# Ordering ScalarE and VectorE by a build-time clock model, with a whole-bank copy and later store transposes

## The chip, the core and the metric

The kernel runs on one core of a Trainium2 chip. Its engines are TensorE (PE, matmuls; PEld is its weight load), VectorE (DVE), ScalarE (ACT), GpSimd (POOL) and SyncE (SP, which here only issues DMAs). Each engine takes its instructions strictly in the order in which the program lists them, and waits on semaphores for the others. The metric is the time of one execution on the device, in microseconds.

## What is computed

```python
# x: (4, 4096, 192) -> 16384 tokens of 192 numbers
out = einsum(softmax(weight) over 7 taps, x padded in front)   # causal, per head
x1 = square(relu(out @ moe_w_in)) @ moe_w_out                  # d_ff = 2048
h2 = x1 @ moe2_w_in
y  = maximum(0.01 * h2, h2) @ moe2_w_out
```

A short convolution over the sequence is followed by two feed-forward layers of the same shape. Layer 1 has relu and square between its matrix products, layer 2 a leaky relu.

## The kernel before

**Tiles and steps.** The 16384 tokens are 32 tiles of 512 (`TT`). A *step* is one layer, one tile and one pair of 128-wide slices of d_ff: `steps[s] = (u, p)` with `u = (layer, tile)` and p from 0 to 7. There are 512 steps. Up to step 47 the kernel also decodes the weights; from step 48 (`THREE`) all steps have one pattern, and from step 64 a period of 32 steps repeats: 16 of layer 1 (two tiles of 8 steps), then 16 of layer 2 for the same two tiles.

**Numbers in two parts.** Matmuls run in a reduced format, so every operand is held as a high and a low part: `hi` is the rounded value, `lo` what is left. From step 48 on, both low parts of a pair are also added up (`both`, made by `add_low`, L619), which saves a matmul.

**What a step does.** TensorE makes two `h` banks of the step (18 matmuls) and, in three blocks of six between them, the 18 output matmuls of step s-2 (`LAG = 2`). Each matmul uses 64 of the 128 rows, and two run side by side, so a step is 18 pairs: five pairs of `h`, three of outputs, two of `h`, three of outputs, two of `h`, three of outputs. ScalarE applies the activation twice (`act`, L576 or L578), squares one of the two in layer 1 (`square`, L585) and rounds both (`high`, L603). VectorE squares the other (L583), takes both differences (`low`, L607) and adds them (`add_low`, L619). The output matmuls of step s, two steps later, need `hi`, `lo` and `both`; for even p of an even tile, and odd p of an odd one, the matmul with `both` stands in the first block of three pairs, otherwise in the second (`g2_one`, order `turn`).

**Leaving the banks.** A tile's outputs gather in three of four PSUM banks: M holds 128 of the 192 columns, E and F hold the rest, each half of it for the wrong half of the partitions. When a tile's last output matmuls have been listed (the `alone` case, `evac_one`), ScalarE copies both halves of E (L743, L744) and half of F (L747), and VectorE adds the rest (`add_rest`, L750) and later the main part (`add_main`, L753) into the scratch tile `ring`. The next tile takes the free bank as M, E as its F and F as its E. Its first matmul into the old E stands at the sixth pair of the step after the leaving one, and into the old F at the eleventh.

**Fill-in work.** VectorE also makes the convolution (`xT` transposes L411, taps L433 and L435 into `acc`), the operands of later tiles (`x`, L484) and the transposes of finished tiles for the stores (`y`, L763, L768), each followed by four store DMAs on SP's queue (L797). These stand in queues `prep` and `leave`, each piece with a due step. `pieces` (L1052) takes from them as long as a budget of VectorE time per step lasts (`STEP`, `SHORT`, `budget`), at most two (`many`) a step, and one around a leaving. The main loop calls it between the activations and the rounding of each step, and after a leaving keeps `both` of the step before back (`pending`) until the leaving's instructions stand.

## Time and profile before

| | |
|---|---|
| median of 3 runs | 2125.22 us (2124.95 to 2126.22) |
| the profiled execution | 2129.57 us |
| its span on the core | 2127.9 us |
| TensorE busy | 2080.6 us, 98% |
| VectorE busy | 1641.3 us, 77%, 2575 instructions |
| ScalarE busy | 1469.1 us, 69%, 2700 instructions |
| mean granted TensorE clock | 0.995 of full speed |

The page of the profile gives one execution. TensorE is busy nearly all the time, yet busy time hides small waits, since two matmuls run side by side and a waiting one still counts beside its neighbour. So it is the length of the steps that is to be read: the time from the first `h` matmul of one step to that of the next, which the timeline of TensorE shows, and the length of a stretch of 16 steps that has been cut at such matmuls.

### The profile page before, as it was taken

The numbers are of one execution on the slowest core, as the hardware profiler recorded it, in microseconds if no ns is written. First come the engines' busy times: TensorE is split into PE (matmuls) and PEld (weight loads), VectorE is DVE, ScalarE is ACT, GpSimd is POOL, SyncE is SP. The second block draws the span as 40 slices with busy tenths as digits, with TensorE's granted clock in tenths as the row PEclk, the third lists the DMA queues.
The fourth block names the chain that finished last, engine by engine and source line by source line (L and its number), as shares of the span: only waits on it lengthen the run. The fifth ranks groups of instructions, "written<-read, shape, count | busy, mean of one in ns | idle before, by whom it ended". The sixth has DMA issues, their size and how long they took to land.

```text
span 2127.9 us, 46893 instructions
## 1 busy us (share of the span) xinstructions
PE 2080.6 (98%) x18592; PEld 1946.0 (91%) x18592; DVE 1641.3 (77%) x2575; ACT 1469.1 (69%) x2700; POOL 61.4 (3%) x114
## 2 busy tenths in 40 slices
PE   9999989999999999999999999999999999999998
PEld 5799988999989999898999989999999998989998
DVE  8787768787777878778787787877778787787764
ACT  7787657667676776767667676676767667677674
POOL 2201210000000000000000000000000000000000
PEclk9999999999999999999999999999999999999999
DMA  8531131121212112131121211212121121311110
GB/s 189 145 95 36 24 57 26 40 37 46 39 23 48 29 46 42 20 65 26 36 39 32 51 26 39 38 45 39 24 48 28 46 42 21 65 21 41 24 33 16
DMA packets 232677, 95.07 MB, mean 45 GB/s; under 512 B 203208, under 2 KB 218696, under 8 KB 232456
## 3 DMA queue, kind: packets, MB, share of 16 engines
q1 hardware_dynamic: 229288, 88.90, 21.2%
q0 software_dynamic: 1168, 2.75, 0.6%
q8 instruction: 145, 2.38, 0.5%
q14 instruction: 76, 0.62, 0.1%
q10 hardware_dynamic: 2000, 0.42, 0.1%
HBM read 25.19 MB, written 12.58 MB: 18 GB/s over the span
## 4 chain that ended last, share of the span: by engine, by line
PE 66%; DVE 22%; ACT 7%; issue 4%; DMA 1%; SPq 0%; DVEq 0%; POOL 0%; ACTq 0%
PE h L544 32%; PE o1m L544 12%; PE o0r L544 11%; PE o1r L544 7%; DVE lo L607 6%; PE o0m L544 5%; DVE both L619 4%; DVE g L583 4%; ACT hi L603 3%; DVE acc_b L435 1%; DVE acc_a L435 1%; DVE ring L750 1%; ACT ring L743 1%; ACT zs L744 1%; ACT ring L747 1%
## 5 line engine op out<-in xcount | busy, mean ns | idle before, releaser
L544 PE MATMUL h<-x,w 64*128 64x512 f32 x9216 | 1350.0, 377 | 2.1 <-ACT g L578 0.9
L544 PEld LDWEIGHTS h<-x,w 64*128 64x128 f32 x9216 | 1038.0, 186 | 23.4 <-ACT g L578 1.3
L607 DVE TENSOR_TENSOR lo<-g,hi 128x512 fp32r<-128x512 f32 x1022 | 661.6, 688 | 325.7 <-ACT hi L603 295.6
L603 ACT CAST hi<-g 128x512 fp32r<-128x512 f32 x1020 | 581.5, 620 | 192.0 <-DVE g L583 188.3
L544 PE MATMUL o1m<-hi,w 64*128 64x512 f32 x2044 | 623.3, 382 | 0.5 <-DVE ring L750 0.5
L544 PE MATMUL o0r<-hi,w 64*128 64x512 f32 x1948 | 586.9, 379 | 0.0
L578 ACT ACTIVATE g<-h 128x512 f32<-128x512 f32 x512 | 279.6, 595 | 320.5 <-PE h L544 319.8
L544 PE MATMUL o1m<-both,w 64*128 64x512 f32 x926 | 360.2, 389 | 25.6 <-DVE both L619 24.5
L544 PE MATMUL o0r<-lo,w 64*128 64x512 f32 (+1 forms) x1022 | 383.6, 378 | 0.0
L544 PEld LDWEIGHTS o1m<-hi,w 64*128 64x128 f32 x2044 | 358.1, 186 | 22.3 <-DVE ring L750 0.9
L544 PEld LDWEIGHTS o0r<-hi,w 64*128 64x128 f32 x1948 | 342.7, 186 | 23.5 <-ACT zs L744 3.2
L619 DVE TENSOR_TENSOR both<-lo 128x512 fp32r<-128x512 f32 x463 | 319.9, 691 | 15.0
L544 PE MATMUL o0m<-hi,w 64*128 64x512 f32 x1088 | 324.8, 379 | 1.6 <-DMA hi<-g 1.6
L544 PE MATMUL o1r<-hi,w 64*128 64x512 f32 x1052 | 322.1, 381 | 0.2 <-ACT zs L744 0.2
L576 ACT ACTIVATE g<-h 128x512 f32<-128x512 f32 x512 | 277.3, 591 | 60.1 <-PE h L544 59.3
L544 PEld LDWEIGHTS o1m<-both,w 64*128 64x128 f32 x926 | 172.2, 186 | 64.3 <-DVE both L619 61.5
L544 PE MATMUL o0m<-lo,w 64*128 64x512 f32 x560 | 208.8, 377 | 0.0
L544 PE MATMUL o1r<-lo,w 64*128 64x512 f32 (+1 forms) x526 | 201.8, 384 | 6.0 <-DVE lo L607 6.0
L544 PEld LDWEIGHTS o0m<-hi,w 64*128 64x128 f32 x1088 | 192.3, 186 | 3.9 <-DMA hi<-g 2.0
L544 PEld LDWEIGHTS o1r<-hi,w 64*128 64x128 f32 x1052 | 186.7, 186 | 4.1 <-ACT zs L744 0.6
L544 PEld LDWEIGHTS o0r<-lo,w 64*128 64x128 f32 (+1 forms) x1022 | 187.0, 183 | 3.6
L585 ACT ACTIVATE g<-g 128x512 f32<-128x512 f32 x269 | 169.0, 631 | 7.8
(136 smaller groups left out, 1333.4 us busy)
## 6 DMA issues: line engine op xcount, KB each, us to landing
x<-x SPq DMA_DIRECT2D x189, 256.0 KB
out_dram<-y SPq DMA_DIRECT2D x186, 64.0 KB
raw_a<-in_x_dram SPq DMA_DIRECT2D x127, 64.0 KB
raw_b<-in_x_dram SPq DMA_DIRECT2D x62, 64.0 KB
lent<-in_moe_w_out_dram SPq DMA_DIRECT2D x13, 256.0 KB
lent<-in_moe_w_in_dram SPq DMA_DIRECT2D x13, 192.0 KB
lent<-in_moe_w_in_dram SPq DMA_DIRECT2D x13, 128.0 KB
lent<-in_moe_w_out_dram SPq DMA_DIRECT2D x13, 128.0 KB
```

Of the source, the lines that this page charges most:

```text
L435: nc.vector.scalar_tensor_tensor(out=acc[0], in0=src, scalar=w, in1=acc[0], op0=ALU.mult, op1=ALU.add)
L544: return nc.tensor.matmul(out=o.rearrange("p (b a) -> p b a", a=2), lhsT=w, rhs=z.rearrange("p (a b) -> p b a", a=2), start=begin, stop=end_,)
L576: nc.scalar.activation(out=g, in_=hps.pop((u, f)), func=ACTF.Relu)
L578: nc.scalar.activation(out=g, in_=hps.pop((u, f)), func=ACTF.Prelu, alpha=0.01)
L583: nc.vector.tensor_mul(out=g, in0=g, in1=g)
L585: nc.scalar.activation(out=g, in_=g, func=ACTF.Square)
L603: nc.scalar.copy(out=a, in_=gsp[u, f])
L607: nc.vector.tensor_sub(out=b, in0=gsp.pop((u, f)), in1=f32(hi[u, f]))
L619: nc.vector.tensor_add(out=c, in0=f32(lo[u, 2 * p]), in1=f32(lo[u, 2 * p + 1]))
L743: nc.scalar.copy(out=z3[w], in_=E[v])
L744: nc.scalar.copy(out=got["s"][v], in_=E[w])
L747: nc.scalar.copy(out=z3[v], in_=F[w])
```

## The change

The order of ScalarE's and VectorE's instructions from step 48 on (the 49th) no longer comes from the budget but from a function `single`. It keeps one clock for each of the two engines, in nanoseconds, and a time `begun` at which TensorE would begin the step if it never waited (18 pairs of 215.6). It knows when `h`, E and F would be ready, lists the step's chain of instructions with 545 on ScalarE, 615 on VectorE and 70 from one to the next, and before every VectorE instruction of the chain calls `fill`, which takes pieces from the same queues as long as the chain's end, `both`, stays before `by`, a time 250 ahead of its matmul; a piece that is not due is taken only if the chain's end moves by no more than 40.

Beside this, `both` belongs to the chain of its own step and is no longer held back. E is copied whole, with one ScalarE instruction in place of two, and F's half goes straight to its place in `ring`; `add_main` is two VectorE instructions of 64 partitions in place of one of 128. The leaving's copies stand between the activations. The store transposes of layer 2 are due two steps later than before (`LEAVE + 2`), though a piece may be taken early.

```diff
+PAIR = 215.6
+STEP_ = 18 * PAIR
+ON_A, ON_D, LATENCY = 545, 615, 70
...
         def early():
-            got["s"] = f32(stage.tile([P, NW], I32, tag="m", name="zs")[:, 0:TT])
-            nc.scalar.copy(out=z3[w], in_=E[v])
-            nc.scalar.copy(out=got["s"][v], in_=E[w])
+            nc.scalar.copy(out=z3, in_=E)
 
         def other():
-            nc.scalar.copy(out=z3[v], in_=F[w])
+            nc.scalar.copy(out=z[v], in_=F[w])
 
         def add_rest():
-            nc.vector.tensor_add(out=zr[v], in0=F[v], in1=got["s"][v])
+            nc.vector.tensor_add(out=zr[v], in0=F[v], in1=z3[w])
 
         def add_main():
-            nc.vector.tensor_add(out=z, in0=M, in1=z3)
+            nc.vector.tensor_add(out=z[w], in0=M[w], in1=z3[v])
+            nc.vector.tensor_add(out=z[v], in0=M[v], in1=z[v])
...
+        def fill(s, chain, at, by, scalar=0):
+
+            while True:
+                best = None
+                for q in (leave, prep, dec):
+                    if not q or (q[0][3] and not q[0][3]()):
+                        continue
+                    cost = q[0][1]
+                    if cost < 0 and not scalar:
+                        continue
+                    if cost > 0:
+                        end = ends(chain, cost, at)
+                        if end > (by if q[0][0] <= s else min(by, ends(chain, 0, at) + 40)):
+                            continue
...
+        def single(s, begun, A, Z, leaving, then, alone):
...
+            at = {"h": begun + 5 * PAIR + 2 * (3 + COVER) * PAIR + 300}
+            first = min(j for order in turns_of(p) for j, k in enumerate(order) if k == (1 if (u[1] % 2 == 0) else 2))
+            by = begun + 2 * STEP_ + (5 + 3 * first + COVER * first + 2) * PAIR - 250
+            names = ("actZ", "actA") if l == 1 else ("actA", "actZ")
+            chain = [(names[0], "A", ON_A, ("h",)), (names[1], "A", ON_A, ("h",))]
+            if l == 1:
+                chain += [("sqZ", "D", ON_D, ("actZ",)), ("sqA", "A", ON_A, ())]
+            chain += [("hiA", "A", ON_A, ("actA",)), ("hiZ", "A", ON_A, ("sqZ", "actZ"))]
+            chain += [("loA", "D", ON_D, ("hiA",)), ("loZ", "D", ON_D, ("hiZ",)), ("c", "D", ON_D, ("loZ",))]
...
+            if alone:
+                early, other, add_rest = leaving
+                at["E"], at["F"] = begun + STEP_ - 3 * PAIR + 300, begun + STEP_ + 300
+                chain = [("e", "A", ON_A, ("E",)), chain[0], ("f", "A", ON_A, ("F",)), ("z", "D", ON_D, ("F", "e"))] + chain[1:]
...
+            if three:
+                begun += STEP_
...
+                then = single(s, begun, A, Z, leaving, then if leaving else (), alone)
+                release()
+                if leaving:
+                    own = (2, u2[1]) if u2[0] == 1 else None
+                    wait = LEAVE if u2[0] == 1 else LEAVE + 2
...
-                if three:
-                    (pending.append if soon else lambda fn: fn())(lambda u=u, p=p: add_low(u, p))
```

TensorE's order of instructions is the same in both kernels. VectorE lists 60 instructions more and ScalarE 60 fewer.

**VectorE at a leaving in layer 1.** Steps 128 and 129 (step 129 is a leaving one), from just behind the `xT_b` transpose. `g` is the square, `lo` the differences, `ring<-o0r` is `add_rest`, `ring<-o1r` is `add_main`, `acc_b` a tap. Before:

```order
L583 TENSOR_TENSOR g<-g 128x512
L433 TENSOR_SCALAR acc_b<-xT_b,taps 128x512
L435 SCALAR_TENSOR_TENSOR acc_b<-xT_b,taps,acc_b 128x512
L607 TENSOR_TENSOR lo<-g,hi 128x512 x2
L750 TENSOR_TENSOR ring<-o0r,zs 64x512
L619 TENSOR_TENSOR both<-lo 128x512
L583 TENSOR_TENSOR g<-g 128x512
L435 SCALAR_TENSOR_TENSOR acc_b<-xT_b,taps,acc_b 128x512
L607 TENSOR_TENSOR lo<-g,hi 128x512 x2
L619 TENSOR_TENSOR both<-lo 128x512
L753 TENSOR_TENSOR ring<-o1r,ring 128x512
L763 STREAM_TRANSPOSE y<-ring 128x512
```

Now:

```order
L435 TENSOR_SCALAR acc_b<-xT_b,taps 128x512
L585 TENSOR_TENSOR g<-g 128x512
L609 TENSOR_TENSOR lo<-g,hi 128x512 x2
L621 TENSOR_TENSOR both<-lo 128x512
L437 SCALAR_TENSOR_TENSOR acc_b<-xT_b,taps,acc_b 128x512 x2
L750 TENSOR_TENSOR ring<-o0r,ring 64x512
L585 TENSOR_TENSOR g<-g 128x512
L609 TENSOR_TENSOR lo<-g,hi 128x512 x2
L621 TENSOR_TENSOR both<-lo 128x512
L753 TENSOR_TENSOR ring<-o1r,ring 64x512
L754 TENSOR_TENSOR ring<-o1r,ring 64x512
```

`both` of step 128 has moved from behind `add_rest` to before two taps and `add_rest`, and the store transpose has moved away from here, to step 132.

**ScalarE at the same place.** `ring<-o1m` is the copy of E, `ring<-o0r` that of F's half, `g<-h` the activations, `hi` the rounding. Before:

```order
L603 CAST hi<-g 128x512 x2
L743 COPY ring<-o1m 64x512
L744 COPY zs<-o1m 64x512
L747 COPY ring<-o0r 64x512
L576 ACTIVATE g<-h 128x512 x2
L585 ACTIVATE g<-g 128x512
```

Now:

```order
L744 COPY ring<-o1m 128x512
L578 ACTIVATE g<-h 128x512
L747 COPY ring<-o0r 64x512
L578 ACTIVATE g<-h 128x512
L587 ACTIVATE g<-g 128x512
L605 CAST hi<-g 128x512 x2
```

One copy has gone, and the first activation has moved ahead of F's copy.

**VectorE at the first store transpose of tile 2 of layer 2, steps 58 and 59.** `ring<-o0m` is `add_main`, `y` the store transpose, whose tile is one buffer that the stores of the tiles before still read. Before:

```order
L619 TENSOR_TENSOR both<-lo 128x512
L753 TENSOR_TENSOR ring<-o0m,ring 128x512
L763 STREAM_TRANSPOSE y<-ring 128x512
L607 TENSOR_TENSOR lo<-g,hi 128x512 x2
L619 TENSOR_TENSOR both<-lo 128x512
L435 SCALAR_TENSOR_TENSOR acc_a<-xT_a,taps,acc_a 128x512 x2
```

Now:

```order
L621 TENSOR_TENSOR both<-lo 128x512
L753 TENSOR_TENSOR ring<-o0m,ring 64x512
L754 TENSOR_TENSOR ring<-o0m,ring 64x512
L609 TENSOR_TENSOR lo<-g,hi 128x512 x2
L621 TENSOR_TENSOR both<-lo 128x512
L764 STREAM_TRANSPOSE y<-ring 128x512
L486 TENSOR_TENSOR x<-acc_a,x 128x512
L609 TENSOR_TENSOR lo<-g,hi 128x512 x2
L621 TENSOR_TENSOR both<-lo 128x512
```

The transpose has moved behind one step's `lo` and `both`; the taps that stood here are done earlier (five of them in step 48).

## Rows read from the trace of the kernel before

**Rows 1.** Waits, whole run: us in total, times, longest us.
```profile
DVE ring L750 <- ACT ring L747: 104.9, 60, 3.9
PEld o1m L544 <- DVE both L619: 61.5, 104, 0.9
PE o1m L544 <- DVE both L619: 24.5, 65, 0.5
```
**Rows 2.** Stretches (from:to, length, busy by engine, clock): layer 1, one and sum of 14.
```profile
562.27:628.53 66.26, 64.85 (x579) 59.49 (x577) 56.27 (x90) 48.06 (x88) 0.00 (x0) 1.00 0.20 34
...
sum 925.06, PE 905.98 PEld 832.95 DVE 776.40 ACT 673.74 POOL 4.98; mean PE 64.71 PEld 59.50 DVE 55.46 ACT 48.12 POOL 0.36
```
**Rows 3.** The same view: layer 2, sum of 14 (steps 80 to 510).
```profile
sum 880.32, PE 873.81 PEld 849.70 DVE 622.21 ACT 575.24 POOL 0.00; mean PE 62.41 PEld 60.69 DVE 44.44 ACT 41.09 POOL 0.00
```
**Rows 4.** The same view: eight steps (147 to 154), step 60, step 61.
```profile
641.07:672.23 31.16, 31.16 (x292) 30.54 (x290) 22.48 (x36) 21.54 (x41) 0.00 (x0) 1.00 0.22 52
278.50:291.15 12.65, 6.61 (x39) 5.18 (x37) 6.61 (x10) 2.70 (x7) 1.64 (x3) 0.74 0.40 79
291.15:295.20 4.05, 4.05 (x38) 3.57 (x36) 3.37 (x5) 2.13 (x5) 0.84 (x3) 0.96 0.20 22
```
**Rows 5.** Timeline of TensorE, steps 128 to 130: start, duration, instruction.
```profile
562.27 1.32 PE L544 MATMUL h<-x,w 64*128 64x512 f32 x10
...
564.51 0.38 PE L544 MATMUL o1m<-hi,w 64*128 64x512 f32 x1
...
570.06 1.32 PE L544 MATMUL h<-x,w 64*128 64x512 f32 x10
...
572.42 0.48 PE L544 MATMUL o1m<-both,w 64*128 64x512 f32 x1 [0.47 <-DVE both L619]
...
574.84 1.32 PE L544 MATMUL h<-x,w 64*128 64x512 f32 x10
```
**Rows 6.** Timeline of ScalarE, the leaving of step 129.
```profile
569.26 0.58 ACT L743 COPY ring<-o1m 64x512 f32<-64x512 f32 x1 [0.69 <-PE o1m L544]
...
570.34 0.58 ACT L747 COPY ring<-o0r 64x512 f32<-64x512 f32 x1
```
**Rows 7.** Timeline of VectorE, the same leaving.
```profile
570.95 0.69 DVE L750 TENSOR_TENSOR ring<-o0r,zs 64x512 f32<-64x512 f32 x1 [1.23 <-ACT ring L747]
571.67 0.69 DVE L619 TENSOR_TENSOR both<-lo 128x512 fp32r<-128x512 f32 x1
```
**Rows 8.** Timeline of TensorE, beginning of step 143.
```profile
624.64 0.43 PE L544 MATMUL h<-x,w 64*128 64x512 f32 x2
```
**Rows 9.** Timeline of VectorE, `both` of step 143.
```profile
631.75 0.69 DVE L619 TENSOR_TENSOR both<-lo 128x512 fp32r<-128x512 f32 x1
```
**Rows 10.** Timeline of VectorE, steps 59 to 60.
```profile
284.35 0.71 DVE L763 STREAM_TRANSPOSE y<-ring 128x512 f32<-128x512 f32 x1 [8.51 <-DMA x<-x]
284.99 1.25 DVE L607 TENSOR_TENSOR lo<-g,hi 128x512 fp32r<-128x512 f32 x2
286.27 0.69 DVE L619 TENSOR_TENSOR both<-lo 128x512 fp32r<-128x512 f32 x1
286.88 1.53 DVE L435 SCALAR_TENSOR_TENSOR acc_a<-xT_a,taps,acc_a 128x512 f32<-128x512 f32 x2
288.33 1.29 DVE L607 TENSOR_TENSOR lo<-g,hi 128x512 fp32r<-128x512 f32 x2
```
**Rows 11.** Timeline of SP's queue, the stores of the first pair of tiles.
```profile
245.98 33.04 SPq L797 DMA_DIRECT2D out_dram<-y  x12
```
**Rows 12.** Groups of instructions: busy us, mean ns of one, idle before.
```profile
L835 ACT COPY ring<-o0m 128x512 f32<-128x512 f32 x2 | 1.2, 585 | 3.4 <-PE o0m L544 3.2 <-PE o1m L544 0.2
```
**Rows 13.** Timeline of SP's queue, end of a period.
```profile
674.64 8.79 SPq L797 DMA_DIRECT2D out_dram<-y  x4
683.48 5.78 SPq L391 DMA_DIRECT2D raw_b<-in_x_dram  x4
```
**Rows 14.** Timeline of VectorE, the transpose that needs `raw_b`.
```profile
695.11 0.71 DVE L411 STREAM_TRANSPOSE xT_b<-raw_b 128x512 f32<-128x512 f32 x1
```

More of the change, by code (lines that the diff above doesn't have):

```diff
@@ L710, in paired, with turns_of @@
         yield
+    def turns_of(p):
+        return ((0, 1, 2), (1, 2, 0)) if p % 2 == 0 else ((2, 1, 0), (0, 2, 1))
     def g2_one(u, p):
@@ L1152, in begin_g1, with on, ends @@
             return [g1(u, p), 9]
+        clock = {"D": 0, "A": 0}
+        def on(engine, took, after=0):
+            clock[engine] = max(clock[engine], after) + took
+            return clock[engine] + LATENCY
+        def ends(chain, extra, at):
+            now_, done = dict(clock), {}
+            now_["D"] += extra
+            for name, engine, took, needs in chain:
+                start = max([now_[engine]] + [done.get(n, at.get(n, 0)) for n in needs])
+                now_[engine] = start + took
+                done[name] = now_[engine] + LATENCY
+            return now_["D"]
@@ L1154, in conv_moe_moe2_kernel @@
         prep_next = 2
-        late, pending = [], deque()
+        begun = 0
+        late = []
         left_at = -2
@@ L1216, in conv_moe_moe2_kernel @@
                 continue
-            soon = s + 1 >= LAG and steps[s + 1 - LAG][1] == NP - 1 and steps[s + 1 - LAG][0] not in in_pair
             if leaving:
```

67 lines of the change are left out of this document (56 added, 11 removed).

## Prediction

> **What bounds the kernel now.** I first read the waits of the whole run [rows 1]. TensorE's own waits go to one releaser: `both`, in 65 waits of its matmuls and 104 of its weight loads. Those sums are no price, because two matmuls run side by side and a late pair also delays the next, so I price by the length of stretches. Eight steps without such a wait last 31.16 us, 3.895 each [rows 4]. The 14 stretches of 16 layer-1 steps last 925.06 us together [rows 2]; 14 x 16 x 3.895 = 872.48, so they lose 52.6. The 14 layer-2 stretches (13 of 16 steps, one of 15) last 880.32 [rows 3] against 223 x 3.895 = 868.59, and lose 11.7. A third loss happens once: step 60 lasts 12.65 and step 61 4.05 [rows 4], 8.9 over two normal ones. All together that is 73.2 us, and the granted clock is 1.00 in all of these stretches but the last.
>
> The timelines show why. Step 130 begins at 570.06 and its matmul with `both` starts at 572.42, after idle time that `both` ended [rows 5]. That operand belongs to step 128, and its `lo` stand ahead of `add_rest` in the order; but `both` stands behind `add_rest`, which waits for ScalarE's copy of F (570.34, 0.58 long), itself behind two copies of E [rows 6, 7]. So `both` ran from 571.67 to 572.36, and TensorE took it at 572.42. The step lasted 4.78 us (570.06 to 574.84 [rows 5]), 0.89 too much. In layer 2 this place, once in 16 steps, is nearly the whole loss: 14 x 0.89 = 12.5, against 11.7 by stretches. In layer 1 it comes on top of other late `both`s, which taps and transposes ahead of the chain cause: 52.6/14 = 3.8 us a stretch, where VectorE is busy for 56.27 of 66.26 us [rows 2].
>
> **The change part by part.**
>
> *The order by clocks.* I follow a layer-1 step that nothing disturbs: step 143 begins at 624.64 and its `both` starts at 631.75 [rows 8, 9], 7.11 after the beginning, and is done at 7.80. It is wanted two steps later, at 7.79 plus seven pairs of 3.895/18 = 0.216, so at 9.30, or at 10.39 if it stands in the second block. That leaves 1.5 or 2.6 us, two or three VectorE instructions. By the new order every layer-1 step carries one tap, and the steps with more have them behind `both`, which is where the spare time lies.
>
> The tightest place is the leaving, steps 128 to 130. VectorE's instruction starts follow each other by 0.61 (286.27 to 286.88), two dependent taps by 1.45 (286.88 to 288.33), a transpose by 0.64 (284.35 to 284.99) [rows 10]. Step 128 has `both` at 7.11. In step 129's time (less 3.895) that is 3.22; taps 3.83, `add_rest` 5.28, the square 5.9. ScalarE copies E at 3.1 (569.26 [rows 6] is 6.99 after step 128's beginning at 562.27 [rows 5], so 3.1 after step 129's), activates at 3.7, copies F at 4.2, activates at 4.8, squares at 5.4, rounds at 6.0 and, when VectorE's square is done at 6.6, at 6.65. Then `lo` 6.65 and 7.3, `both` 8.0 to 8.7, wanted at 10.4. In step 130: `both` of 129 at 4.1, the two halves of `add_main` 4.7 and 5.3, square 5.95 to 6.65, last rounding to 7.3, `lo`, and `both` at 8.1 to 8.8, wanted at 9.3. Step 131 is back at 7.1. The same sum for the other leaving, where a tap, a small copy (0.2) and a transpose stand ahead (0.67 + 0.2 + 0.64 = 1.51 in place of 1.45), gives `both` 0.06 later. No wait is left there, so I take the 52.6 + 11.7 = **64.3 us** as gone. The bound on the other side is that each place still waits (first rival).
>
> *What becomes late next: the old F.* The next tile's first matmul into it stands 2.24 after step 130's beginning (564.51 less 562.27, the same matmul in an undisturbed step [rows 5]). It waits for `add_rest`, which starts at 5.28 less 3.895 = 1.39 and ends 0.69 later at 2.08; at the other leaving 2.14. That is in time by 0.1, but not by the 0.2 that a weight load goes ahead; a matmul that had to wait takes 0.48 in place of 0.38 [rows 5]. I take 0.05 on average for 28 leavings in layer 1, **+1.4 us**. Bounds: 0, and 0.89 each (a step such as 130), +24.9.
>
> *The whole copy of E.* ScalarE takes 0.58 for 64 partitions [rows 6] and 0.585 for 128 [rows 12], so a copy of about 0.58 goes from each of 60 leavings, ahead of F's copy. F's last matmul starts just before step 130's beginning at 570.06 and lasts 0.38, so its copy cannot start much before 570.3 in either kernel [rows 5, 6]; the shorter copy only lets an activation go ahead of it, which is in the chain above, and brings 0 by itself. At the very end of the kernel the copies and adds are a chain: ScalarE saves 0.6 and VectorE's added half costs 0.6, so I take 0.
>
> *`add_main` in halves.* VectorE takes 0.69 for 64 partitions (`add_rest`) and 0.69 for 128 (`both`) [rows 7], so a half costs a whole: 0.61 of issue time at 59 places, 36 us, at no cost as long as VectorE has idle time there. In layer 1, 16 steps hold 90 VectorE instructions now as 91 in the list before, some 55.9 us of 62.3 at the issue times of rows 10, or 90%: that is the cover, and it costs 0. The Trainium skill, "Perfetto Trace Analysis", section "Optimizing Scalar/DVE Operations", says that grouping work into larger operations helps if an engine is saturated, which speaks against the split; the same section says that breaking up helps where the engine is not saturated and makes others wait. By the first the layer-1 term would be lost (rival 2); by the second it stands.
>
> *The store transpose at step 59.* Twelve stores of the first pair hold SP's queue from 245.98 to 279.02 [rows 11]; the next transpose writes the tile that they read, and starts at 284.35 after 8.51 of idle time [rows 10]. Nothing here makes the stores earlier, so it will start at 284.35 again. But it now stands behind step 58's `lo` and `both`, so step 60 runs undisturbed until 282.4, and TensorE waits for the first `lo` of step 59, seven pairs into step 61, at 283.9. Behind the transpose stand one `x` and the `lo`: 284.99 + 0.61 = 285.6, done at 286.3, so 2.4 us of waiting, then some 0.2 for `both` and 0.2 each for two new starts: 3.0 in place of 8.9, **-5.9 us**. The clock matters here: it was 0.74 on average over step 60 [rows 4], that is half speed for some 6.6 us, after 6 us without matmuls, and half of those 6.6 were lost. If it falls again, the gain is 2.5. I take 5.9, since the wait is 2.4 and not 6; bounds 2.5 and 8.9. The Trainium skill, "TensorE: Matmul & The Clock Gate", Part 1, says that an array that sat idle falls to half its clock; if this wait counts as that, the 2.5 holds.
>
> *Taps moved to step 48.* Five taps, some 3.6 us, now stand ahead of `lo` of step 48 and of the bank copy of the pair that leaves in step 49. VectorE waits there before; I take **+0.4 us**, between 0 and 0.9.
>
> **Sum:** -64.3 + 1.4 - 5.9 + 0.4 = -68.4. Against the profiled execution's 2129.57 (span 2127.9) this gives 2061.2; the median of the runs is 4.35 lower, and the same saving gives 2125.2 - 68.4 = **2057 us**.
>
> **The rivals.**
> 1. *The bank takes the place of `both`.* Pieces stand ahead of `add_rest`, and the clocks bound only `both`, not the old F. For: 0.1 us of room. Against: the sum above. With 0.89 at each of 28 leavings, 2057 + 23.5 = 2080.
> 2. *VectorE is full in layer 1.* With issue times over 10% above those of rows 10 the chain slips from step to step, and the layer-1 gain goes: 2057 + 52.6 = 2109. Against: the pieces are costed in the clocks at 700 or 750, above the 0.61 to 0.73 that the rows show.
> 3. *Slower: a VectorE instruction that waits for a DMA in every period.* The transpose of `raw_b` starts at 695.11 [rows 14]; the loads are issued until 689.26, behind four stores that begin at 674.64 [rows 13]. The store transpose now stands behind a `both`, and the stores begin some 1.4 us later. If loads land as late as the stores of rows 11 did (279.02 to 284.35, 5.3 us), the transpose waits 0.9, which `both`'s 1.5 of room hides. It decides from about 1.5 + 64.3/14 = 6 us of waiting a period; a wait as at step 59 (8.9 a period, 13 periods) gives 2057 + 116 = 2173.
> 4. *The change does not do what it says:* the `both`s are in time and TensorE waits as long for something that the releasers hid (`hi`, or the turns of two halves on a bank). Then 2125.
>
> **How the numbers follow.** The forecast 0.70, rival 1 0.14, rival 2 0.08, rival 3 0.04, rival 4 0.04. What a measurement of this kernel can tell from no change is about 0.2%, 4 us. The forecast and rivals 1 and 2 are all faster by more: 0.92; within 0.2%: 0.04; slower: 0.04. The range reaches down to 2048 (all 73.2 gone, and steps at the 3.885 of the shortest ones, another 4) and up to 2080, rival 1; the cases beyond hold 0.16, and the forecast's own case nearly all lies within.
>
> **What would show it.** Right: layer-1 stretches of 16 steps at 62.2 to 62.6 us and layer-2 ones at 62.2 to 62.4; `both` all but gone from TensorE's waits; a transpose into `y` that still waits until about 284, with step 61 some 3 us long over the rest, and the clock at full or half speed behind it. Wrong: steps of 4.4 or more at the leavings with `add_rest` as the releaser (rival 1), VectorE without idle time in layer 1 (rival 2), a DMA ahead of `xT_b` (rival 3), stretches as long as before (rival 4).

## The result, and the profile after

The changed kernel takes **2068.68 us** (median of 4 runs, 2067.77 to 2070.02) against 2125.09 for the kernel before in the same comparison (4 runs): a ratio of 0.9734, 95% interval 0.9717 to 0.9751. That is 56.4 us less. The forecast was 2057, with a range of 2048 to 2080: the direction and the place were right, and 12 of the 68 us forecast did not come.

The profiled execution of the changed kernel took 2070.02 us, its span is 2068.3. Line numbers have moved by two or so: `both` is L621, `lo` L609, the matmuls L546, `add_rest` L750, the halves of `add_main` L753 and L754. First the waits of the whole run (us in total, times, longest), which answer [rows 1]:

```profile
DVE ring L750 <- ACT ring L747: 10.2, 7, 3.7
...
PEld o1m L546 <- DVE both L621: 3.8, 3, 3.2
...
PEld o1m L546 <- DVE ring L750: 3.3, 12, 0.9
...
PEld o0r L546 <- DVE ring L750: 3.1, 13, 0.4
...
PE o1m L546 <- DVE both L621: 2.8, 1, 2.8
```

TensorE's waits for `both` have gone from 65 and 104 to one and three. What stands in their place is `add_rest`, 25 times a weight load and never more than 0.9 us. VectorE itself, which stood 104.9 us behind ScalarE's copy of F, now stands 10.2.

The stretches of 16 steps (from:to, length, busy time of PE, PEld, DVE, ACT, POOL, clock) answer [rows 2] and [rows 3]. Layer 1, one stretch and the sum of the same 14:

```profile
546.14:609.10 62.96, 62.96 (x580) 61.17 (x578) 55.69 (x88) 48.61 (x86) 0.00 (x0) 1.00 0.22 39
...
sum 880.47, PE 880.35 PEld 856.32 DVE 771.08 ACT 680.15 POOL 5.17; mean PE 62.88 PEld 61.17 DVE 55.08 ACT 48.58 POOL 0.37
```

and layer 2, the sum of 14:

```profile
sum 871.75, PE 871.58 PEld 851.75 DVE 677.68 ACT 564.26 POOL 0.00; mean PE 62.26 PEld 60.84 DVE 48.41 ACT 40.30 POOL 0.00
```

Layer 1 fell from 925.06 to 880.47, by 44.6 us; layer 2 from 880.32 to 871.75, by 8.6. Against steps of 3.895 the first still loses 8.0 (880.47 less 872.48), the second 3.2 (871.75 less 868.59). Nearly all steps from 64 on now take 3.88 to 3.90. Forty do not: three in each period of 32 but the last, steps such as 130, 138 and 154, at 4.25, 4.21 and 4.14, and one more in the first. The timeline of TensorE over step 130 (start, duration, instruction) answers [rows 5]:

```profile
553.92 1.32 PE L546 MATMUL h<-x,w 64*128 64x512 f32 x10
...
556.08 0.39 PE L546 MATMUL o1m<-hi,w 64*128 64x512 f32 x1
556.40 0.48 PE L546 MATMUL o0r<-hi,w 64*128 64x512 f32 x1
...
558.17 0.45 PE L546 MATMUL h<-x,w 64*128 64x512 f32 x2
```

The first matmul into the old F, `o0r<-hi`, starts 2.48 into the step (556.40 less 553.92); 2.24 was the place of that matmul in a step that nothing delays [rows 5]. It starts behind `add_rest`, which VectorE's timeline shows:

```profile
553.48 0.69 DVE L621 TENSOR_TENSOR both<-lo 128x512 fp32r<-128x512 f32 x1
554.09 1.53 DVE L437 SCALAR_TENSOR_TENSOR acc_b<-xT_b,taps,acc_b 128x512 f32<-128x512 f32 x2
555.65 0.69 DVE L750 TENSOR_TENSOR ring<-o0r,ring 64x512 f32<-64x512 f32 x1
```

`add_rest` runs from 555.65 to 556.34, 1.73 to 2.42 into the step. Two taps stand ahead of it. This is what the first rival of the prediction said, at some 0.3 a time in place of its 0.89.

The loss at the twelve stores is the other place, in windows of steps 60 and 61 (columns as above), VectorE's and then TensorE's timeline, as in [rows 4] and [rows 10]:

```profile
274.60:278.50 3.90, 3.90 (x39) 3.75 (x37) 0.00 (x0) 2.11 (x5) 0.61 (x3) 1.00 0.31 46
278.50:287.24 8.74, 5.92 (x40) 4.74 (x37) 5.08 (x8) 2.11 (x5) 0.98 (x4) 0.80 0.87 172
```

```profile
279.80 0.71 DVE L764 STREAM_TRANSPOSE y<-ring 128x512 f32<-128x512 f32 x1 [5.58 <-DMA x<-x]
...
282.33 0.69 DVE L621 TENSOR_TENSOR both<-lo 128x512 fp32r<-128x512 f32 x1
```

```profile
283.07 0.76 PE L546 MATMUL o1m<-both,w 64*128 64x512 f32 x1 [2.82 <-DVE both L621]
```

Step 60 is whole again (3.90), step 61 takes 8.74: 12.64 for the two in place of 16.70.

At the end of the kernel VectorE's timeline shows the last sums, now three:

```profile
2056.67 0.69 DVE L750 TENSOR_TENSOR ring<-o0r,ring 64x512 f32<-64x512 f32 x1 [3.66 <-ACT ring L747]
2057.37 0.68 DVE L753 TENSOR_TENSOR ring<-o1r,ring 64x512 f32<-64x512 f32 x1
2058.07 0.69 DVE L754 TENSOR_TENSOR ring<-o1r,ring 64x512 f32<-64x512 f32 x1
```

The last step took 17.04 us up to TensorE's last instruction, 15.49 before. All terms together: -44.6 and -8.6 in the layers, -4.1 at steps 60 and 61, +0.5 at step 50, +1.6 at the end, in sum -55.2. The spans of the two profiles differ by 4.4 us more, in steps 0 to 47, which the change does not touch: from TensorE's first matmul to step 48 they lasted between 225.1 us (experiment 5) and 230.3 (the kernel before) in the fourteen profiles of this study.

### The profile page after: what moved, and what is told of

The parts are those of the page before. It is cut to its first block, busy times and chain, and to the rows that moved or that the text cites. A ratio compares the mean times of both kernels' runs of the same rounds, so it can differ in the third digit from the quotient of the medians.

```text
span 2068.3 us, 46894 instructions
## 1 busy us (share of the span) xinstructions
PE 2052.0 (99%) x18592; PEld 1974.9 (95%) x18592; DVE 1694.8 (82%) x2635; ACT 1463.7 (71%) x2640; POOL 66.0 (3%) x114
## 3 DMA queue, kind: packets, MB, share of 16 engines
q0 software_dynamic: 1168, 2.75, 0.7%
## 4 chain that ended last, share of the span: by engine, by line
PE 94%; DVE 3%; ACT 1%; DMA 1%; issue 1%; SPq 0%; DVEq 0%; POOL 0%; ACTq 0%
PE h L546 46%; PE o1m L546 16%; PE o0r L546 15%; PE o0m L546 8%; PE o1r L546 8%; DVE lo L609 1%; ACT hi L605 0%; DVE acc_b L437 0%; DMA w<-in_moe_w_out_dram 0%; DMA x<-x 0%; DVE acc_a L437 0%; DMA hi<-g 0%; ACT g L578 0%; ACT x L511 0%; DVE lent L270 0%
## 5 line engine op out<-in xcount | busy, mean ns | idle before, releaser
L546 PE MATMUL h<-x,w 64*128 64x512 f32 x9216 | 1350.0, 376 | 1.2 <-ACT g L580 0.5
L546 PEld LDWEIGHTS h<-x,w 64*128 64x128 f32 x9216 | 1063.1, 186 | 9.6 <-ACT g L580 0.9
L609 DVE TENSOR_TENSOR lo<-g,hi 128x512 fp32r<-128x512 f32 x1022 | 668.2, 689 | 302.5 <-ACT hi L605 283.8
L605 ACT CAST hi<-g 128x512 fp32r<-128x512 f32 x1020 | 590.0, 620 | 61.1 <-DVE g L585 50.0
L546 PE MATMUL o1m<-hi,w 64*128 64x512 f32 x2044 | 622.0, 381 | 0.9 <-DVE ring L750 0.7
L546 PE MATMUL o0r<-hi,w 64*128 64x512 f32 x1948 | 590.0, 380 | 0.1
L580 ACT ACTIVATE g<-h 128x512 f32<-128x512 f32 x512 | 282.9, 595 | 318.6 <-PE h L546 317.8
L546 PE MATMUL o0r<-lo,w 64*128 64x512 f32 (+1 forms) x1022 | 382.3, 376 | 0.0
L546 PEld LDWEIGHTS o1m<-hi,w 64*128 64x128 f32 x2044 | 358.0, 186 | 25.2 <-DVE ring L750 3.3
L578 ACT ACTIVATE g<-h 128x512 f32<-128x512 f32 x512 | 282.1, 594 | 133.4 <-PE h L546 130.9
L546 PEld LDWEIGHTS o0r<-hi,w 64*128 64x128 f32 x1948 | 343.3, 186 | 21.4 <-DVE ring L750 3.1
L546 PE MATMUL o1m<-both,w 64*128 64x512 f32 x926 | 349.0, 377 | 2.8 <-DVE both L621 2.8
L621 DVE TENSOR_TENSOR both<-lo 128x512 fp32r<-128x512 f32 x463 | 320.5, 692 | 18.0
L546 PE MATMUL o0m<-hi,w 64*128 64x512 f32 x1088 | 324.5, 378 | 0.0
L546 PE MATMUL o1r<-hi,w 64*128 64x512 f32 x1052 | 318.6, 378 | 0.0
L546 PE MATMUL o0m<-lo,w 64*128 64x512 f32 x560 | 208.3, 377 | 0.0
L546 PE MATMUL o1r<-lo,w 64*128 64x512 f32 (+1 forms) x526 | 198.2, 377 | 0.0
L546 PEld LDWEIGHTS o0m<-hi,w 64*128 64x128 f32 x1088 | 191.9, 186 | 1.4 <-POOLq L660 0.3
L546 PEld LDWEIGHTS o0r<-lo,w 64*128 64x128 f32 (+1 forms) x1022 | 186.8, 183 | 0.6
L546 PEld LDWEIGHTS o1r<-hi,w 64*128 64x128 f32 x1052 | 186.2, 186 | 1.1
L546 PEld LDWEIGHTS o1m<-both,w 64*128 64x128 f32 x926 | 172.4, 186 | 4.4 <-DVE both L621 3.8
```

The source lines that it names most:

```text
L546: return nc.tensor.matmul(out=o.rearrange("p (b a) -> p b a", a=2), lhsT=w, rhs=z.rearrange("p (a b) -> p b a", a=2), start=begin, stop=end_,)
L578: nc.scalar.activation(out=g, in_=hps.pop((u, f)), func=ACTF.Relu)
L580: nc.scalar.activation(out=g, in_=hps.pop((u, f)), func=ACTF.Prelu, alpha=0.01)
L605: nc.scalar.copy(out=a, in_=gsp[u, f])
L609: nc.vector.tensor_sub(out=b, in0=gsp.pop((u, f)), in1=f32(hi[u, f]))
L621: nc.vector.tensor_add(out=c, in0=f32(lo[u, 2 * p]), in1=f32(lo[u, 2 * p + 1]))
```

## The experiments

The kernel before is timed again beside each kernel, so ratios are compared, not times. A change of 0.001 in a ratio is 2.1 us.

**1. The order without the new copies.** The first question was which of the edits does the work.

```diff
         def early():
-            nc.scalar.copy(out=z3, in_=E)
+            got["s"] = f32(stage.tile([P, NW], I32, tag="m", name="zs")[:, 0:TT])
+            nc.scalar.copy(out=z3[w], in_=E[v])
+            nc.scalar.copy(out=got["s"][v], in_=E[w])
...
         def add_main():
-            nc.vector.tensor_add(out=z[w], in0=M[w], in1=z3[v])
-            nc.vector.tensor_add(out=z[v], in0=M[v], in1=z[v])
+            nc.vector.tensor_add(out=z, in0=M, in1=z3)
...
-                chain = [("e", "A", ON_A, ("E",)), chain[0], ("f", "A", ON_A, ("F",)), ("z", "D", ON_D, ("F", "e"))] + chain[1:]
+                chain = [("e", "A", 2 * ON_A, ("E",)), chain[0], ("f", "A", ON_A, ("F",)), ("z", "D", ON_D, ("F", "e"))] + chain[1:]
```

The copy of F's half (into `z3` again) and `add_rest` (from `zs` again) go back with it.

> The changed kernel with the bank copies of before: E is copied in two halves (one into `zs`), `add_main` is one instruction again; the new order of ScalarE and VectorE stays, with the copy of E costed at twice the time in the model of the clocks. Theory: the order alone brought the gain, and the whole copy and the split cost nothing between steps 48 and 510, so 2066 to 2072, with the layer-1 stretches at 62.6 to 63.4 us and the last step near the 15.49 of before in place of 17.04. Rival: the shorter copy chain at the leavings is what frees `both`; then 2085 or more, and `both` is back among TensorE's waits at the second step after each leaving.

Measured: 2092.49 us, ratio 0.9831 (0.9817 to 0.9846). The theory fell, and the time is that of the rival: 20.6 us of the 56 (0.9831 less 0.9734, of 2125) are missing without the new copies. But `both` is not the releaser, as the rival had it. TensorE's waits name `add_rest` (L754 in this kernel):

```profile
PE o0r L546 <- DVE ring L754: 9.5, 13, 0.9
PE o1m L546 <- DVE ring L754: 7.1, 14, 0.8
```

and VectorE's timeline of step 130, which begins at 556.94, shows why:

```profile
557.11 2.32 DVE L437 SCALAR_TENSOR_TENSOR acc_b<-xT_b,taps,acc_b 128x512 f32<-128x512 f32 x3
559.46 0.69 DVE L754 TENSOR_TENSOR ring<-o0r,zs 64x512 f32<-64x512 f32 x1
```

Three taps stand ahead of `add_rest` where two stood, since the model was told of a longer copy and so sees VectorE idle for longer. So two prices are mixed here, that of the longer copy and that of the third tap. Experiment 12 separates them.

**2. The new copies without the order.** The diff is that of the copies in the change, put into the kernel before.

```diff
-            got["s"] = f32(stage.tile([P, NW], I32, tag="m", name="zs")[:, 0:TT])
-            nc.scalar.copy(out=z3[w], in_=E[v])
-            nc.scalar.copy(out=got["s"][v], in_=E[w])
+            nc.scalar.copy(out=z3, in_=E)
...
-            nc.vector.tensor_add(out=z, in0=M, in1=z3)
+            nc.vector.tensor_add(out=z[w], in0=M[w], in1=z3[v])
+            nc.vector.tensor_add(out=z[v], in0=M[v], in1=z[v])
```

> The kernel before with the new bank copies alone: E whole, `add_main` in two halves, the order as it was. Theory: nothing gained, 2125 to 2135, since `both` is held behind `add_rest` all the same, F's copy cannot start before F is finished, and VectorE has one instruction more at each leaving; layer-1 stretches at 66 us or more. Rival: the copy frees the leavings, 2115 or less.

Measured: 2141.8 us, ratio 1.0065 (1.005 to 1.008): slower, by 14. The layer-1 stretches (sum of 14, as [rows 2]) hold it all; the layer-2 ones are at 880.31, as before:

```profile
sum 940.39, PE 910.15 PEld 835.65 DVE 798.22 ACT 659.25 POOL 5.37; mean PE 65.01 PEld 59.69 DVE 57.02 ACT 47.09 POOL 0.38
```

940.39 less 925.06 is 15.3, or 1.1 a stretch, and VectorE is busy for 1.6 us more in each (57.02 less 55.46). Step by step, two things of opposite sign add up to it. The second step behind each leaving is 0.7 longer (132: 4.87 for 4.17, 140: 4.61 for 3.88), and step 141 by 0.1: in the old order the half of `add_main` was not free in layer 1. But the step behind the second leaving is shorter (138: 3.97 for 4.43), since F's copy comes earlier there. ScalarE's timeline of step 138, of the kernel before (step from 603.41) and of this one (from 604.02):

```profile
604.55 0.58 ACT L747 COPY ring<-o1m 64x512 f32<-64x512 f32 x1
...
604.58 0.58 ACT L743 COPY ring<-o1m 64x512 f32<-64x512 f32 x1
```

That is 1.14 into the step and then 0.56. At step 130 the copy starts 0.27 into the step in both kernels, so there the shorter copy of E brings nothing. One and the same edit costs 14 us in the old order and, by experiment 1, is worth 20 in the new one.

**3. Only the held-back `both` let go.** In the kernel before, one line:

```diff
-    (pending.append if soon else lambda fn: fn())(lambda u=u, p=p: add_low(u, p))
+    add_low(u, p)
```

> The kernel before, with `both` issued behind its own `lo` at every step: it is no longer held back until `add_rest` has been issued at the second step of a leaving. Nothing else is changed. Theory: this place alone is worth 14 x 0.84 = 11.7 us in layer 2 and 14 x 0.89 = 12.4 in layer 1, so 2101, give or take 4, with the layer-2 stretches at 62.1 to 62.4 and the layer-1 ones at 65.2; TensorE's waits on `both` stay in layer 1. Rival: the late `add_rest` then keeps the old F, and the same time is lost there: 2121 to 2129. A second rival: nearly all of the gain hangs on this place, through steps behind it: 2080 or less.

Measured: 2104.1 us, ratio 0.9887 (0.9871 to 0.9904), 24.0 us less: the theory, whose sum was 24.1. Layer 1 (first) and layer 2, sums of 14:

```profile
sum 915.07, PE 899.75 PEld 836.15 DVE 779.55 ACT 669.27 POOL 5.96; mean PE 64.27 PEld 59.73 DVE 55.68 ACT 47.80 POOL 0.43
...
sum 867.99, PE 867.99 PEld 850.50 DVE 622.29 ACT 575.59 POOL 0.00; mean PE 62.00 PEld 60.75 DVE 44.45 ACT 41.11 POOL 0.00
```

Layer 2 loses nothing any more, by a change of one line; layer 1 gained 10.0. `add_rest` keeps no one waiting there: in the kernel before it began 0.89 into step 130 (570.95 [rows 7]), since the copy of F comes ahead of the activations. The rest of the layer-1 loss (915.07 less 872.48, 42.6) needs the new order.

**4. `add_rest` first.** In the changed kernel:

```diff
-    if engine == "D":
+    if engine == "D" and name != "z":
         fill(s, chain, at, by, 1 if name == "loA" else 0)
```

> The changed kernel with one thing different: no tap or transpose stands ahead of `add_rest` on VectorE at a leaving; they come behind it. Theory: the 11 to 12 us that the steps at the leavings still lose (three steps in 32 of 4.14 to 4.25 us) are TensorE's wait for the old F, and go: 2057 to 2060, with those steps at 3.9 to 4.0. Rival: the pieces that move behind `add_rest` make `both` late by as much, and the time stays at 2066 to 2071, with `both` as the releaser.

Measured: 2071.63 us, ratio 0.9735 (0.9721 to 0.975), the same as the changed kernel: the rival. In step 130 VectorE now waits for ScalarE's copy:

```profile
555.41 0.69 DVE L750 TENSOR_TENSOR ring<-o0r,ring 64x512 f32<-64x512 f32 x1 [0.66 <-ACT ring L747]
```

Windows of steps 130 and 132 (lengths in the second place) show that the wait went from the first to the second:

```profile
554.50:558.40 3.90, 3.90 (x39) 3.75 (x37) 3.20 (x6) 3.58 (x7) 0.00 (x0) 1.00 0.02 4
562.29:566.87 4.58, 4.33 (x40) 3.77 (x38) 4.10 (x7) 3.77 (x7) 0.00 (x0) 1.00 0.00 0
```

Step 132, 3.90 in the changed kernel, is 0.68 longer here, with `both` as the releaser. The 0.66 us of idle time ahead of `add_rest` is about one VectorE instruction (0.61 to 0.78 from start to start) that is then missing behind it. In layer 2, where VectorE has time to spare, the same edit did take the wait away: 868.36 in place of 871.75.

**5. The store transpose of step 59 at its due step.**

```diff
+    if q is leave and q[0][4] is None and q[0][0] > s:
+        continue
```

> The changed kernel, with store transposes that have no store tile of their own given out only from the step at which they are due, never as early filling. The one of step 59 moves behind the twelve stores and nothing else is altered on purpose; later ones move by a step or two with it. Theory: the 4.84 us that step 61 loses are this transpose, so it goes to 3.9 and the granted clock stays at 1.00 from step 60 to 63: 2064 (ratio 0.971). Rival: the transpose merely waits at another step for the same store queue and the loss comes back there: 2068.

Measured: 2069.0 us, ratio 0.9727 (0.9713 to 0.9742): the rival. The edit did more than the theory counted on: it also held back the first pair's own three transposes (steps 54 and 55), so the twelve stores began at 254.33 instead of 241.45, in SP's queue:

```profile
254.33 33.05 SPq L798 DMA_DIRECT2D out_dram<-y  x12
```

and the next transpose met them all the same, at step 64:

```profile
292.39 0.71 DVE L764 STREAM_TRANSPOSE y<-ring 128x512 f32<-128x512 f32 x1 [7.56 <-DMA out_dram<-y]
```

Here the profile names the stores as what it waited for, where the other two kernels have a DMA of `x`. It starts 5.0 us after the queue is through with the stores (287.38); in the changed kernel it was 5.3 (274.50 to 279.80), in the kernel before 5.3 [rows 10, 11]. What counts is the distance between the first pair's transposes and the next one, not the next one alone. Experiment 10 makes that distance longer.

**6. `add_main`'s half twice.** One more VectorE instruction at each leaving of the changed kernel, which the planner does not know of.

```diff
     nc.vector.tensor_add(out=z[w], in0=M[w], in1=z3[v])
+    nc.vector.tensor_add(out=z[w], in0=M[w], in1=z3[v])
```

> The changed kernel with the first half of `add_main` done twice: one more VectorE instruction of 0.7 us at every leaving, behind `add_rest` and ahead of the next step's square; the model of the clocks is not told. It measures the cover on which the split was costed at nothing. Theory: VectorE has no spare time in the two steps behind a leaving in layer 1 (`both` of step 130 starts 0.74 into step 132 and is wanted some 0.7 later), so 0.6 us at each of 28 leavings in layer 1 and nothing in layer 2: 2080 to 2086, with `both` back among TensorE's waits. Rival: VectorE is busy for 82% of the span and its idle time hides it: 2067 to 2071.

Measured: 2083.97 us, ratio 0.9795 (0.9781 to 0.981), 13 us more than the changed kernel; 2080 to 2086 was the theory. It is all in layer 1 (892.78, 12.3 more; layer 2 871.46, no more):

```profile
sum 892.78, PE 889.12 PEld 847.46 DVE 786.39 ACT 681.66 POOL 4.60; mean PE 63.51 PEld 60.53 DVE 56.17 ACT 48.69 POOL 0.33
```

A stretch lost 0.88 us: 0.71 in the second step after the first leaving (132) and 0.17 at the second one (141), where the theory had 0.6 at each. So at the first place an instruction costs its full time, although VectorE is busy for 88% of a layer-1 stretch (55.69 of 62.96) and 82% of the span. The Trainium skill, "Perfetto Trace Analysis", section "Optimizing Scalar/DVE Operations", makes it depend on saturation whether grouping or splitting pays; the runs agree, if one reads saturation in the two steps behind a leaving and not as a share of a stretch.

**7, 8, 9. The model's durations, and one piece ahead of `add_rest`.** Two edits, each alone and both together. The first sets the model to the distance from start to start that the trace shows; the second allows at most one tap or transpose ahead of `add_rest`.

```diff
-ON_A, ON_D, LATENCY = 545, 615, 70
+ON_A, ON_D, LATENCY = 600, 640, 70
...
+    if cost > 300 and most <= 0:
+        continue
...
-    fill(s, chain, at, by, 1 if name == "loA" else 0)
+    fill(s, chain, at, by, 1 if name == "loA" else 0, 1 if name == "z" else 99)
```

The durations alone:

> The changed kernel with the model's durations set to what the trace shows from one start to the next: ScalarE 600 in place of 545, VectorE 640 in place of 615. Theory: two steps behind the leavings lose their early pieces, but at step 130 two taps still stand ahead of `add_rest`, and at step 146 now three, so the old F is waited for at these: 0.35 and about 0.7 us, 14 times each, against 0.3 and 0.25 gained at steps 138 and 154: 2069 to 2078. Rival: the durations are all that was wrong, and every wait goes: 2057 or less.

Measured: 2070.02 us, ratio 0.973 (0.9715 to 0.9744). The theory in its lower part: step 138 is whole, 130 is as it was, and step 146 (beginning at 616.75) has three taps ahead of `add_rest`, in VectorE's timeline:

```profile
616.31 2.32 DVE L437 SCALAR_TENSOR_TENSOR acc_a<-xT_a,taps,acc_a 128x512 f32<-128x512 f32 x3
618.66 0.69 DVE L750 TENSOR_TENSOR ring<-o0r,ring 64x512 f32<-64x512 f32 x1
```

Both together:

> As the run before, and with at most one tap or transpose ahead of `add_rest` at a leaving. VectorE then has one instruction while ScalarE copies F, and `add_rest` starts when the copy ends, about 0.95 into the step. Theory: old F and `both` are then both in time, and the 11 to 12 us lost at the leavings go: 2056 to 2060, steps of 3.9 throughout from 64 on. Rival: VectorE is too full at the leavings of layer 1 for any order, and the waits stay on `both`: 2066 or more.

Measured: **2057.16 us**, ratio 0.9671 (0.9655 to 0.9687). From step 64 on every step but the last takes 3.88 to 3.91; the sums of the stretches, layer 1 and layer 2, reach those of the prediction's ideal (872.48 and 868.59):

```profile
sum 872.28, PE 872.28 PEld 854.96 DVE 726.91 ACT 678.16 POOL 5.41; mean PE 62.31 PEld 61.07 DVE 51.92 ACT 48.44 POOL 0.39
...
sum 868.40, PE 868.40 PEld 851.08 DVE 719.65 ACT 563.90 POOL 0.00; mean PE 62.03 PEld 60.79 DVE 51.40 ACT 40.28 POOL 0.00
```

In step 130, which begins at 551.88, VectorE does one tap while ScalarE copies F (552.18 to 552.76), and `add_rest` follows at once, the next tap behind it:

```profile
552.04 0.75 DVE L438 SCALAR_TENSOR_TENSOR acc_b<-xT_b,taps,acc_b 128x512 f32<-128x512 f32 x1
552.82 0.69 DVE L751 TENSOR_TENSOR ring<-o0r,ring 64x512 f32<-64x512 f32 x1
```

With its durations longer, the model also puts other work behind `both` where it stood ahead: at the first leaving `add_main` goes from step 131 to step 132, and some 42 to 44 us of VectorE's work move from the layer-1 stretches (771.08 to 726.91) to the layer-2 ones (677.68 to 719.65), where it had time to spare.

One piece alone:

> The changed kernel with at most one tap or transpose ahead of `add_rest` at a leaving, and the model's durations as they were. It completes the square of two edits: neither, each alone, both. Theory: both are needed. The old F is in time now (0.35, 0.3 and 0.25 us less at steps 130, 138 and 154), but the tap that moved behind `add_rest` and the two halves of `add_main` stand ahead of `both` of step 130, which then starts 1.09 into step 132 instead of 0.74 and is late by some 0.3, and likewise at step 139 or 140: 28 times 0.3 back, so 2064 to 2068. Rival: the one piece alone was the fault: 2056 to 2060.

Measured: 2061.69 us, ratio 0.9693 (0.9677 to 0.971), better than the changed kernel and than the durations alone. The time lies between the theory's range and the rival's. The old F is in time, and `both` is late at one step of a period (132, 4.12), not at two; the theory had the mechanism and a price more than twice too high (8.4 us for 3.1 in layer 1: 875.38 here, 872.28 in experiment 8). By the ratios this line brings 8.7 us and the durations on top of it 4.7, of which the stretches show the 3.1; the durations alone brought 0.9, which the intervals do not tell from nothing.

**10. The store transpose later, the first pair's early.** On experiment 8:

```diff
+    if q is leave and s > 55 and q[0][4] is None and q[0][0] > s:
+        continue
```

> The run with the measured durations and one piece ahead of `add_rest` (2057.16 us), and in it store transposes without a tile of their own are taken early only up to step 55: the first pair's three stay as early as they are there, the one of step 61 moves to step 63, where it is due. Theory: the twelve stores are then done before it (their queue starts as early as in that run, unlike in the run where all transposes were moved), and the 4.2 us that steps 61 and 62 lose go: 2053, step 63 within 0.2 of 3.9, granted clock 1.00 from step 56 to 64. Rival: the store queue ends after step 63 has begun and the wait comes back: 2055 or more.

Measured: 2055.61 us, ratio 0.9663 (0.9648 to 0.9677). Steps 61 to 63 take 3.88 to 3.90, so the 4.2 us are gone from there, as the theory said; but the median fell by only 1.6, to a time that the rival had named for another reason. The last step of the profiled execution took 17.04 where that of experiment 8 took 15.83, which gives 1.2 back; the other 1.4 are within the intervals.

**11. The last sums in another order.** On experiment 10, in the last evacuation alone, the half of `add_main` that needs only E goes ahead:

```diff
         early()
         other()
+        half_e, half_f = then[0].halves
+        half_e()
         add_rest()
-        then[0]()
+        half_f()
```

> As the run before, and in the last evacuation the half of `add_main` that needs only E stands ahead of `add_rest`, in the time in which ScalarE copies F. VectorE's last sum of the tail then ends 0.7 us earlier (10.8 into the last step in place of 11.5). Theory: 0.7 us off the last step at the least, and up to 1.1 more or less by where the granted clock falls in the idle time ahead of the last transposing matmuls: 2051 to 2053. Rival: the chain through F's copy sets the end, and nothing changes: 2053.

Measured: **2052.05 us**, ratio 0.9647 (0.9633 to 0.9662), the fastest kernel of this study. VectorE's timeline of the end, to hold against the three sums of the changed kernel above:

```profile
2039.96 0.68 DVE L754 TENSOR_TENSOR ring<-o1r,ring 64x512 f32<-64x512 f32 x1 [2.91 <-ACT ring L745]
2040.71 0.69 DVE L751 TENSOR_TENSOR ring<-o0r,ring 64x512 f32<-64x512 f32 x1
2041.42 0.70 DVE L757 TENSOR_TENSOR ring<-o1r,ring 64x512 f32<-64x512 f32 x1
```

The last sum ends 0.7 earlier in the step, and the step takes 15.11 in place of 17.04. The order of the sums gives 0.7 of these 1.9 us; the rest goes with the place where the clock fell, which the last section shows.

**12. The old copies with one piece ahead.** The diff of experiment 1 on the kernel of experiment 8, cut to its main lines.

```diff
-            nc.scalar.copy(out=z3, in_=E)
+            got["s"] = f32(stage.tile([P, NW], I32, tag="m", name="zs")[:, 0:TT])
+            nc.scalar.copy(out=z3[w], in_=E[v])
+            nc.scalar.copy(out=got["s"][v], in_=E[w])
...
-            nc.vector.tensor_add(out=z[w], in0=M[w], in1=z3[v])
-            nc.vector.tensor_add(out=z[v], in0=M[v], in1=z[v])
+            nc.vector.tensor_add(out=z, in0=M, in1=z3)
```

> The run with the measured durations and one piece ahead of `add_rest` (2057.16 us), with the bank copies of before in it: E in two halves, `add_main` in one. In the run with the old copies in the changed kernel a third tap had come ahead of `add_rest` as well, so the price of the longer copy and that of the tap were mixed; here at most one piece can stand there, and what is left is the copy. Theory: the second copy of E puts F's copy 0.7 later, at 1.0 to 1.6 into the step, `add_rest` runs from 1.62 to 2.31, and the old F is wanted at 2.24, so 0.2 to 0.35 at each of 56 leavings: 2068 to 2077, with `add_rest` among TensorE's releasers. Rival: the planner's third tap was all, and the whole copy is worth nothing by itself, as the prediction had it: 2055 to 2060.

Measured: 2074.78 us, ratio 0.9755 (0.9739 to 0.9771), 17.8 us more than experiment 8. Step 130 begins at 553.88; ScalarE's timeline, then VectorE's:

```profile
553.67 0.58 ACT L749 COPY zs<-o1m 64x512 f32<-64x512 f32 x1
554.27 0.60 ACT L579 ACTIVATE g<-h 128x512 f32<-128x512 f32 x1
554.89 0.58 ACT L752 COPY ring<-o0r 64x512 f32<-64x512 f32 x1
```

```profile
554.06 0.74 DVE L438 SCALAR_TENSOR_TENSOR acc_b<-xT_b,taps,acc_b 128x512 f32<-128x512 f32 x1
555.50 0.69 DVE L755 TENSOR_TENSOR ring<-o0r,zs 64x512 f32<-64x512 f32 x1 [0.69 <-ACT ring L752]
```

The second copy of E pushes the activation and F's copy 0.7 later, VectorE stands idle for 0.69, and `add_rest` ends 2.31 into the step. All four leavings of a period lose 0.24 (steps of 4.14), 57 of them 13.7 us, and the rest is in steps behind them in layer 1. So the whole copy, with the split that it brings, is worth 18 us in this order, with no third tap in it (one piece stands ahead of `add_rest` at step 130, none at the other three). The theory holds; the rival, which was the prediction's own term, falls. Two ways around were not tried: the old copies with F's copy ahead of both activations, as in the kernel before, and an `add_rest` that does not wait for F's copy, though by the code it reads the other half of F and nothing that this copy writes.

## Why the prediction was right, and where it was off

**That the order by clocks takes the waits on `both` away: right.** It was forecast at -64.3 with 1.4 back for the old F; it measured 53.2 (44.6 and 8.6). Experiment 3 gave 24.0 us for the held-back `both`, where the rows had given 24.1 (by stretches 10.0 and 12.3, for 12.4 and 11.7), and experiment 8 shows that the ideal on which the 64.3 rests can be reached, so the bound of TensorE at 3.895 a step was read rightly. The changed kernel itself did not reach it: its layer-1 stretches take 62.9 us on average (880.47 by 14) and most layer-2 ones 62.5, where the prediction named 62.2 to 62.6 and 62.2 to 62.4 as the sign of being right.

**The old F: the term that was mis-sized.** It was put at 1.4 and measured 11.2: 8.0 in layer 1 and 3.2 in layer 2, where the prediction had none. The step that failed is the chain of starts. It put `add_rest` at 1.39 into step 130; it starts at 1.73. Of these 0.34, 0.23 come from the step that was taken as the example. Step 143's `both` starts 7.11 after the step's beginning, but step 143 was cleaner than its neighbours: VectorE's square was done (629.45) before ScalarE came to the rounding (629.79). Step 142 of the same trace begins at 620.76, and there the rounding (626.08) follows the end of the square (626.04); its `both` stands here, in VectorE's timeline of the kernel before:

```profile
628.05 0.69 DVE L619 TENSOR_TENSOR both<-lo 128x512 fp32r<-128x512 f32 x1
```

This is 7.29, and the changed kernel's step 128 has 7.34 (553.48 less 546.14). The other 0.11 is the distance of two taps and `add_rest`: 1.56 (554.09 to 555.65), where two taps ahead of a `lo` had 1.45 [rows 10]. The room at this leaving was 0.16 (2.24 less 2.08): the first error alone was more than that, and the second alone would have left 0.05. In layer 2 no chain had been worked out for the leaving at all: the sum was made for 28 leavings of layer 1, and step 154 has two taps ahead of `add_rest` as well.

**The bounds saved the range.** The prediction kept 0.89 for each of 28 leavings as the far end, and rival 1 at 2080 with a chance of 0.14. The truth lies between: 40 steps at 0.28 on average (11.2 by 40). So the place and the mechanism are the rival's, the time is nearer to the forecast's, and a mixture of the two had no case of its own.

**The whole copy at nothing: the reason was wrong, the sum was not hurt.** Experiment 12 prices it at 18 us. The prediction said that F's copy cannot start before F is finished in either kernel. That is so, but it is what holds the copy up only at the leaving that was read (0.27 into step 130); at the other one, in the kernel before, the copies of E hold it up until 1.14 into step 138 (experiment 2). The new order also puts an activation ahead of it, and only the time that the whole copy frees makes that harmless: without it F's copy starts 1.01 into step 130 (554.89 less 553.88). The chain used ScalarE's starts with the short copy in it, so the gain was inside the 64.3 and was not missed.

**`add_main` in halves at nothing: right only with the new order, and by little.** Its cover was argued from a share (90%). In experiment 2 it made the second step behind each leaving 0.7 longer, so that layer 1 lost 15.3 us in spite of the shorter copy, and experiment 6 lost 12.3 by a further half in the new order: the cover behind the first leaving is less than one instruction.

**Steps 59 to 61: -4.1 in place of -5.9.** The transpose started 5.3 after the stores, as forecast, and step 60 ran whole. TensorE waited for `both`, not for the first `lo`, since this tile takes `both` into its first block; the wait was 2.82 in place of 2.4. Then the granted clock fell, which the prediction had kept as its other bound (2.5):

```profile
283.14:286.55 3.41, 3.41 (x16) 2.75 (x18) 1.77 (x3) 0.00 (x0) 0.41 (x2) 0.50 0.81 123
```

3.41 us at half speed lose 1.7; with the 2.82 and new starts that is the 4.84 by which step 61 is too long. Experiment 5 shows the same wait without the clock: TensorE had no matmul from 291.18 to 294.33, 3.15 us, the granted clock stayed at 1.00, and step 64 was 3.5 too long:

```profile
289.43:296.81 7.38, 4.23 (x39) 3.53 (x37) 4.35 (x7) 2.10 (x5) 0.68 (x3) 1.00 0.75 132
```

The sentence from the Trainium skill ("TensorE: Matmul & The Clock Gate", Part 1) that was set against the chosen value agrees with the row of step 61, where the level is 0.50, 1.2 GHz, after 2.82 us without a matmul, and not with the row of experiment 5. What decides between the two was not tried.

**Taps at step 48: +0.5 for +0.4.** **The end of the kernel: +1.6 for 0.** "ScalarE saves 0.6" was wrong: F's copy waits for F, and moved only from 9.10 to 8.83 into the last step. VectorE's last sum ends 0.43 later: the second half of `add_main` puts 0.70 on it, and the earlier copy takes 0.27 off. The other 1.1 goes with the place where the clock fell (last section).

**Rivals 2, 3 and 4** did not come. Layer 1 has idle time on VectorE, the transposes of `raw_b` wait 0.2 us in the whole run, and the waits on `both` went. But rival 2 names what decides at the leavings, for two steps instead of sixteen.

## What to carry to other kernels

Work out a chain from the ordinary step, not from the cleanest one; where the room is 0.1 us, take the start from three places of the trace and use the latest. A planner that fills idle time needs every deadline of the work behind it: here the model bounded `both` and not the bank that `add_rest` frees, and one more rule (one piece ahead) with durations from the trace brought 11.5 us by the medians. An edit that moves a wait is tried both ways, with and without its partner: the new copies cost 14 us alone and were worth 18 with the order.

## What the runs showed of the hardware

The end of the kernel varies by more than its instructions. In the fourteen profiles TensorE stands idle for 2.2 to 3.6 us ahead of the last transposing matmuls, and the granted clock falls to 0.50 (1.2 GHz) somewhere behind that idle time's beginning, not at a fixed place in the program. In the changed kernel it fell at 2058.07, 0.8 us ahead of these matmuls, so all of them ran at half speed (windows of the idle time and of what follows):

```profile
2056.02:2058.07 2.05, 0.00 (x0) 0.00 (x0) 1.38 (x2) 0.58 (x1) 0.00 (x0) 1.00 0.00 0
2058.07:2064.90 6.83, 5.40 (x16) 4.00 (x16) 1.25 (x2) 0.48 (x1) 0.00 (x0) 0.50 0.10 30
```

In experiment 11 they began at 2042.21, before it fell at 2043.9:

```profile
2039.00:2043.54 4.54, 2.39 (x16) 1.53 (x13) 2.07 (x3) 1.16 (x2) 0.00 (x0) 1.00 0.00 0
2043.54:2047.00 3.46, 2.84 (x10) 2.02 (x10) 0.56 (x1) 0.48 (x1) 0.00 (x0) 0.55 0.17 57
```

The last step took 15.1 to 17.5 us over the fourteen kernels, one profiled execution of each, and neither set of copies holds one end: 17.04 and 15.79 (the changed kernel, experiment 2) with the new ones, 15.49 and 16.61 (the kernel before, experiment 3) with the old. In the changed kernel and in experiment 2 VectorE's last sum ends at the same place of the step (11.54) and TensorE's idle time is the same (2.85), so those 1.25 us are not the instructions'. Why the clock falls where it does was not tried, so of the +1.6 at the end only the 0.43 on VectorE is laid to the change.

Twelve stores take SP's queue 33.05 us, 2.75 each, in each of the traces shown here (33.04 to 33.05), and the tile they read is free 5.0 to 5.3 us after the last. A transpose that needs the tile has to stand that far behind.
